# Lightning attention and a low-rank mixer: v's loads on another queue, V's second copy by DMA, some work on other engines and in other steps

## The chip, the cores and the metric

One core of a Trainium2 chip runs the whole kernel. The core has a matmul engine (PE; its weight loads are listed as PEld), a vector engine (DVE, VectorE), a scalar engine (ACT, ScalarE), GpSimd (POOL), and SyncE (SP), which only issues DMAs here. ScalarE can issue DMAs too; each of the two has a queue of its own to the same 16 DMA engines. Times are device microseconds of an execution; lower is better.

## The reference

Inputs: q, k and v of shape (4, 8, 768, 64) in float32, a decay `lam` for each of 8 heads, and U (768 x 32), V (32 x 768), w1 (512 x 2048), w2 (2048 x 512) in float64.

```python
# attention, blocks of 64 positions, per batch and head
intra = ((qb @ kb.T) * Dmask) @ vb          # Dmask[i, j] = lam ** (i - j), i >= j
inter = (qb * lam_pow) @ kv_state
out[block] = intra + inter
kv_state = lam ** 64 * kv_state + (kb * rev_pow).T @ vb
# x: (4, 768, 512), the heads side by side
h = x.transpose(0, 2, 1) @ U @ V            # mixes positions
u = x + h.transpose(0, 2, 1)
result = u + maximum(u @ w1, 0) @ w2
```

## The kernel before, in words

The attention stage runs in 24 steps, one for 128 positions of one batch: step s has batch b = s // 6 and place c = s % 6 in it. The list `pieces` gives the order of the work of all steps, and `run` says what each name does. Every engine takes its instructions in the order in which this list emits them, so the list is the schedule. Steps overlap: step s also turns q and k of step s + 1 (`prep`, L371), computes its scores (`scores`, L403) and masks them on VectorE (`masked`, L413), and finishes step s - 7 (`done`): `mix` (L556) multiplies it with V, `mixed` (L573) adds x, `turn` (L593) transposes the result for the next stage and `store` (L590) writes it to DRAM.

The middle of a step is `intra` (px, L459), `state` (pkv, L431) and `inter` (L470), after which ScalarE copies the result out of PSUM (x_nat, L476). In steps up to 6 `state` comes before `intra`. PSUM has one px tile in this stage, so the next `intra` follows this copy.

Loads run ahead of their use: `prep(s)` ends with the request for the next q, `next_v(s)` (L447), between `state` and `inter`, with the next v, and the end of each step with the next k. There are three buffers each for q and v and four for k, so a load asked for in a step is read about three steps later. q and k are asked for by SyncE, v by ScalarE (the first two by SyncE). The request waits on its engine until the buffer that it fills has been read; what is queued behind it on that engine waits too.

At the end of each batch, `low` (L481) forms U-transposed x as a 128 x 128 tile with four groups g of 32 rows, `low_rows` (L497) then splits it into a high and a low part that lie in the tile vp (as `p_hl`). Its work for the first three batches is in two pieces that `next_of_low` takes up in the first step of the following batch (steps 6, 12 and 18): `own` casts each group on ScalarE (L529) and subtracts on POOL (L530), `other` has SyncE copy each group's rows to its neighbour by four DMAs (L540). `mix` needs both, for the first time in the step after (7, 13 and 19; there it comes after `inter`).

V itself is prepared once, in steps 0 to 5 (`v_steps`, L699): it is fetched as 64-bit words and turned into float32, `five` cuts the low bits off on VectorE (L716), `high` writes this to groups 0 and 2 of `v_hl` with four ScalarE copies (L723), and `low` writes the differences to groups 1 and 3, two subtractions on VectorE and two on POOL (L727). Groups 2 and 3 (rows 64 to 127) hold the same as groups 0 and 1.

Between these, `aside(s)` emits side work listed in `side`: fetches of w1's words (L146, four pieces of 128 KB for each of the first two blocks) and the steps that turn 64-bit words into float32 parts (`one`, L166, and two activations, L173 and L174; `mantissa`, L155; `two`, L184, and so on). The numbers in the list `at` say in which step. What a side step has for ScalarE is kept by `on_scalar` and emitted later, at `late` (in the next step for most; in steps 5 and 6 right after `inter` and `other`).

After the attention stage come the first product (u with w1, L837 and L848) and the second (L969, L971, L973), which run until the end.

Of the kernel before, what the change touches and what calls it, by code (L numbers as in the profile page):

```python
# [8 lines left out]
FP32 = mybir.dt.float32  # L9
# [3 lines left out]
ALU = mybir.AluOpType  # L13
# [5 lines left out]
def kernel(  # L19
# [28 lines left out]
    nc = tc.nc  # L48
# [8 lines left out]
    R = moe_U.shape[1]  # L57
    G = P // R
    SH = S // 2
    NS = B * NT  # L60
# [43 lines left out]
    def tmp(name):  # L104
        return wconv.tile([P, C], FP32, tag="tmp", bufs=2, name=name)
# [149 lines left out]
    def two_banks(name, tag):  # L255
        return psf.tile([P, 2, N], FP32, tag=tag, name=name)
# [7 lines left out]
    def bank(shape, name, tag):  # L264
        return psa[0].tile(shape, FP32, tag=tag, bufs=2, name=name)
# [5 lines left out]
    def parts(s):  # L271
        return 2 if s == 0 else 1
# [20 lines left out]
    v_hl, p_hl = vp[:, 0:S], vp[:, S : S + C]  # L293
# [46 lines left out]
    half = [slice(0, D), slice(D, P)]  # L340
# [105 lines left out]

    def next_v(s):  # L447
        del raw[s, "v"]
        load_next("v", nc.scalar)

    def intra(s):

# [26 lines left out]
    pps = {}  # L479

    def low(b):  # L481

        pp = two_banks("pp", "px")[:, 0, 0:P] if b < B - 1 else bank([P, P], "pp", "b2")
        for c in range(NT):
            for g in range(G):
                nc.tensor.matmul(  # L486
                    out=pp[g * R : (g + 1) * R, :], lhsT=u_w[:, c, :],
                    rhs=xs[b * NT + c][:, g * P : (g + 1) * P],
                    start=(c == 0), stop=(c == NT - 1),
                )  # L490
        if b == B - 1:
            pps[b] = pp
            return
        pps[b] = tmp("p_f")[:, 0:P]
        nc.scalar.copy(pps[b], pp)

    def low_rows(b):  # L497

        pp = pps.pop(b)
        own = [(slice(g * R, (g + 1) * R), slice(g * P, (g + 1) * P)) for g in range(G)]  # L500
        if b == B - 1:
            h, h2, l, l2 = (p_hl[g * R : (g + 1) * R] for g in range(G))
# [12 lines left out]

            def spread_low():
                nc.scalar.copy(l2, l.bitcast(FP32))

            pps[b] = [low_part, spread, spread_low]
            return  # L520


        def place(g, of, low):
            return p_hl[g * R : (g + 1) * R, low * 2 * P + (of % 2) * P :][:, 0:P]

        def own():
            for g in range(G):
                rows, at = pp[g * R : (g + 1) * R], place(g, g, 0)
                nc.scalar.copy(at, rows)  # L529
                nc.gpsimd.tensor_tensor(  # L530
                    out=place(g, g, 1), in0=rows, in1=at.bitcast(FP32), op=ALU.subtract
                )

        def other():
            for g in range(G):
                at, of = (
                    p_hl[x * R : (x + 1) * R].rearrange("r (l h c) -> r l h c", l=2, h=2)
                    for x in (g ^ 1, g)
                )
                nc.sync.dma_start(  # L540
                    out=at[:, :, g % 2].bitcast(FP32), in_=of[:, :, g % 2].bitcast(FP32)
                )

        pps[b] = [own, other]

    def next_of_low(b):
        pps[b].pop(0)()
# [102 lines left out]
    for s in range(NS):  # L650
        b, c = divmod(s, NT)
        done = s - NT - 1
        more = s + 1 < NS
        turns = done > 0 and (done - 1) // TG < FG
        mixes = 0 <= done < NS - NT - 1
        rows = c == 0 and b > 0
        step = [("fade", s)] * (c > 0)
        step += [("mix", done)] * (mixes and c != 1) + [("turn", done - 1)] * turns
        step += [("split", done - 1)] * turns
        step += [("next_of_low", b - 1)] * (s == NT)  # L660
        step += [("prep", s + 1)] * more
        step += [("mix", done + 1)] * (not more)
        step += [("next_of_low", b - 1)] * (rows and s > NT)
        step += [("scale", s + 1)] * more
        step += [("mixed", done)] * (mixes and c != 1)
        step += [("late", s - 1)] * (1 < s < NT - 1 or s > NT)
        step += [("turned", done - 2)] * (done > 1 and c == 1)
        step += [("mixed", done + 1)] * (not more)
        both = [("intra", s), ("state", s)]
        step += (both if s > NT else both[::-1]) + [("next_v", s), ("inter", s)]  # L670
        step += [("next_of_low", b - 1)] * rows
        step += [("late", s)] * (s < 2 or s in (NT - 1, NT))
        step += [("turned", done - 1)] * (done > 0 and c > 0)
# [25 lines left out]
    def v_steps():  # L699

        st = {}

        def dst():
            if "v" not in st:
                st["v"] = wconv.tile([P, C], FP32, tag="wf", name="vf")[0 : 2 * R, 0:SH]
            return st["v"]

        def parts(gs):
            for half in range(2):
                rows, cols = slice(half * R, (half + 1) * R), slice(half * SH, (half + 1) * SH)  # L710
                for g in gs:
                    yield v_hl[g * R : (g + 1) * R, cols], rows

        def five():
            st["t"] = t = wconv.tile([P, C], FP32, tag="wt", name="vt")[0 : 2 * R, 0:SH]
            nc.vector.tensor_scalar(  # L716
                t.bitcast(U32), st["v"].bitcast(U32), HI, None, ALU.bitwise_and
            )
            on_scalar(high)

        def high():
            for out, rows in parts((0, 2)):
                nc.scalar.copy(out, st["t"][rows])  # L723

        def low(g, engine):
            for out, rows in parts((g,)):
                engine.tensor_tensor(  # L727
                    out=out, in0=st["v"][rows], in1=st["t"][rows], op=ALU.subtract
                )

        halves = [moe_V[:, half * SH : (half + 1) * SH] for half in range(2)]
        return weight_steps(dst, halves, SH, 2 * R, in_parts=True) + [
            five, lambda: low(1, nc.vector), lambda: low(3, nc.gpsimd),
        ]


# [3 lines left out]
    side = {}  # L740
    for steps, at in (
        (u_side, (-1, 1, 1, 2, 2)),
        (v_steps(), (0, 0, 3, 3, 4, 4, 4, 5, 5)),
        (w1_steps(0, True, True), (8, 9, 10, 11, 12, 14, 15, 16, 17, 17, 20, 21)),
        (w1_steps(1, True, True), (14, 15, 16, 17, 18, 22, 23, NS, NS, NS, NS, NS)),
    ):
        assert len(steps) == len(at)
        for step, n in zip(steps, at):
            side.setdefault(n, []).append(step)
# [142 lines left out]
    c0, b = NS - NT, B - 1  # L892
# [7 lines left out]
    at = [(1, 5), (1, 17), (2, 4), (2, 17), (3, 3), (3, 10)]  # L900
# [121 lines left out]
    for i in range(len(steps) - STAG):  # L1022
        g, ft = steps[i]
# [49 lines left out]
```

## Time and profile before

| what | value |
|---|---|
| median of 3 runs | 649.1 us (649.07 to 650.27) |
| the profiled execution | 649.85 us, of which span 648.1 us, granted clock 1.000 |
| attention stage | from 0 to about 114.5 us |
| idle PE before 115 us / between 115 and 400 / after 400 us | 4.9 / 0.0 / 3.8 us |
| a steady step (say 74.51 to 78.83, between two runs of L408) | 4.3 us |
| busy ACT / DVE / POOL, whole span | 268.8 / 434.7 / 116.3 us |
| v loads by ScalarE / by SyncE | 22 / 2, 256 KB each, 4.7 us to landing |
| `other` copies (vp<-vp) | 12, 32 KB each, 2.7 us to landing |

The steps' scores (L408) begin as follows: scores(5) at 28.4 us, (6) at 32.2, (7) at 37.5, (8) at 42.0, (12) at 59.4, (13) at 65.2, (14) at 70.1, (18) at 86.9, (19) at 92.8, (20) at 97.5, (23) at 110.6. scores(s) is emitted in step s - 1.

In a row of the timeline the columns are start, duration, engine, line, operation, output<-inputs, shapes and count; brackets hold the engine's idle time before the row and what ended it. An engine with a q (SPq, ACTq) is its sequencer, which issues DMAs; the duration of an issue includes its waiting. In a row of waits the columns are total us, times and the longest.

### The profile page before, as it was taken

The numbers are of one execution on the slowest core, as the hardware profiler recorded it, in microseconds if no ns is written. First come the engines' busy times: TensorE is split into PE (matmuls) and PEld (weight loads), VectorE is DVE, ScalarE is ACT, GpSimd is POOL, SyncE is SP. The second block draws the span as 40 slices with busy tenths as digits, with TensorE's granted clock in tenths as the row PEclk, the third lists the DMA queues.
The fourth block names the chain that finished last, engine by engine and source line by source line (L and its number), as shares of the span: only waits on it lengthen the run. The fifth ranks groups of instructions, "written<-read, shape, count | busy, mean of one in ns | idle before, by whom it ended". The sixth has DMA issues, their size and how long they took to land.

```text
span 648.1 us, 13405 instructions
## 1 busy us (share of the span) xinstructions
PE 639.3 (99%) x5242; PEld 539.3 (83%) x5242; DVE 434.7 (67%) x709; ACT 268.8 (41%) x500; POOL 116.3 (18%) x104
## 2 busy tenths in 40 slices
PE   9899999999999999999999999999999999999997
PEld 8888989788888888888888888888888888888886
DVE  6656878668997777777796244685575665755854
ACT  3675766435755444444454222332322322322320
POOL 4475968330000000000000000030030300300300
PEclk9999999999999999999999999999999999999999
DMA  9979996354876555655587899864363363543521
GB/s 232 241 182 272 231 242 163 119 191 176 287 258 219 209 207 209 207 209 211 211 292 276 320 332 392 287 220 138 96 227 98 123 204 97 172 152 99 179 82 65
DMA packets 132737, 131.69 MB, mean 203 GB/s; under 512 B 81538, under 2 KB 90754, under 8 KB 132674
## 3 DMA queue, kind: packets, MB, share of 16 engines
q1 hardware_dynamic: 107552, 124.41, 59.1%
q10 hardware_dynamic: 25122, 6.42, 4.4%
q8 instruction: 41, 0.67, 0.4%
q14 instruction: 22, 0.18, 0.1%
HBM read 80.09 MB, written 50.33 MB: 201 GB/s over the span
## 4 chain that ended last, share of the span: by engine, by line
PE 97%; ACT 1%; issue 1%; DMA 1%; DVE 0%; ACTq 0%; DVEq 0%
PE pz L837 27%; PE pd L848 13%; PE pz L971 13%; PE pz L969 13%; PE pd L973 13%; PE px L459 4%; PE pss L408 4%; PE px L470 2%; PE pqk L361 2%; PE pkv L431 1%; PE pm L563 1%; PE pp L486 1%; PE pm L626 1%; DMA kraw<-in_k_dram 1%; PE put L604 1%
## 5 line engine op out<-in xcount | busy, mean ns | idle before, releaser
L837 PE MATMUL pz<-u_hl,w 128*128 128x512 f32 x768 | 185.0, 391 | 0.0
L837 PEld LDWEIGHTS pz<-u_hl,w 128*128 128x128 f32 x768 | 143.7, 188 | 30.2 <-ACT r L844 0.6
L971 PE MATMUL pz<-w_hl,m 128*128 128x512 f32 x384 | 148.7, 389 | 0.0
L969 PE MATMUL pz<-w_hl,m 128*128 128x512 f32 x384 | 148.3, 389 | 0.0
L973 PE MATMUL pd<-w_d,m 128*128 128x512 f32 x384 | 147.4, 389 | 0.0
L952 ACT ACTIVATE m<-rm 128x512 fp32r<-128x512 f32 x96 | 60.6, 632 | 182.3 <-PE pd L973 125.5
L953 DVE SCALAR_TENSOR_TENSOR m<-rm,m 128x512 fp32r<-128x512 f32 x96 | 71.6, 748 | 95.7 <-ACT m L952 95.7
L998 POOL TENSOR_TENSOR o<-o,u 128x512 f32<-128x512 f32 x20 | 29.8, 1523 | 433.1 <-DVE o L994 433.1
L853 DVE SCALAR_TENSOR_TENSOR r<-pd,r 128x512 f32<-128x512 f32 x96 | 61.7, 685 | 60.4 <-ACT r L844 48.2
L848 PE MATMUL pd<-u_d,w 128*128 128x512 f32 x384 | 95.7, 390 | 0.0
L971 PEld LDWEIGHTS pz<-w_hl,m 128*128 128x128 f32 x384 | 72.1, 188 | 15.0
L969 PEld LDWEIGHTS pz<-w_hl,m 128*128 128x128 f32 x384 | 72.1, 188 | 15.0
L973 PEld LDWEIGHTS pd<-w_d,m 128*128 128x128 f32 x384 | 72.1, 188 | 14.7
L848 PEld LDWEIGHTS pd<-u_d,w 128*128 128x128 f32 x384 | 72.0, 188 | 14.9
L844 ACT ACTIVATE r<-pz 128x512 f32<-128x512 f32 x96 | 51.7, 591 | 66.9 <-PE pz L837 66.9
L954 DVE SCALAR_TENSOR_TENSOR m<-m 128x512 fp32r<-128x512 f32 x96 | 74.7, 779 | 3.0
L417 DVE TENSOR_TENSOR sm<-pss,mask 128x512 f32<-128x512 f32 x48 | 30.9, 686 | 18.0 <-PE pss L408 17.8
L215 ACT ACTIVATE w<-wf 128x512 fp32r<-128x512 f32 x32 | 20.3, 633 | 36.5 <-DVE wf L197 28.7
L173 ACT ACTIVATE sc<-sc,ends 128x512 f32<-128x512 uint32 x30 | 21.6, 721 | 22.8 <-DVE sc L166 22.8
L459 PE MATMUL px<-vraw,sm 128*64 128x64 f32 x768 | 29.0, 228 | 1.6 <-issue 1.4
L408 PE MATMUL pss<-qt,kt 64*128 64x128 f32 x384 | 29.0, 290 | 0.6 <-issue 0.5
L459 PEld LDWEIGHTS px<-vraw,sm 128*64 128x64 f32 x768 | 25.9, 140 | 3.4 <-issue 2.5
(91 smaller groups left out, 606.6 us busy)
## 6 DMA issues: line engine op xcount, KB each, us to landing
r_d<-r SPq DMA_DIRECT2D x96, 256.0 KB, 2.5
rm<-r_d SPq DMA_DIRECT2D x96, 256.0 KB, 2.7
words<-in_moe_w_ch_dram SPq DMA_DIRECT2D x30, 512.0 KB, 4.2
w_d<-w SPq DMA_DIRECT2D x16, 768.0 KB, 3.4
w_hl<-w_d SPq DMA_DIRECT2D x16, 512.0 KB, 6.2
u_d<-x_nat SPq DMA_DIRECT2D x24, 256.0 KB, 4.4
u<-u_d SPq DMA_DIRECT2D x24, 256.0 KB, 4.5
qraw<-in_q_dram SPq DMA_DIRECT2D x23, 256.0 KB, 4.8
```

The lines of the kernel that those rows point to most:

```text
L408: nc.tensor.matmul(out=pss[:, x, a, :], lhsT=kt[half[x], a, :], rhs=qt[half[x], a, :], start=True, stop=True,)
L459: nc.tensor.matmul(out=px[half[t], x, a, :], lhsT=sm[:, x, a, half[t]], rhs=vr[:, 2 * a + x, :], start=(a == 0), stop=(alone and a == HP - 1),
L837: nc.tensor.matmul(out=like(acc[g][0], g), lhsT=w[:, n, ct, :], rhs=columns(uhl[g][:, n], g, ct), start=(ct == 0 and n == 0), stop=(ct == ...
L844: nc.scalar.mul(rs[g], acc[g][0], 4096.0 + 1.0)
L848: nc.tensor.matmul(out=like(acc[g][1], g), lhsT=w[:, 2, ct, :], rhs=columns(ud[g], g, ct), start=(ct == 0), stop=(ct == CT - 1),)
L853: nc.vector.scalar_tensor_tensor(rs[g], acc[g][1], 4096.0, rs[g], ALU.mult, ALU.add)
L952: nc.scalar.activation(out=m[:, 0], in_=r, func=AF.Relu, scale=NEAR)
L953: nc.vector.scalar_tensor_tensor(m[:, 1], r, 0.0, hi, ALU.max, ALU.subtract)
L954: nc.vector.scalar_tensor_tensor(m[:, 2], hi, E, low, ALU.mult, ALU.subtract)
L969: nc.tensor.matmul(out=pz, lhsT=m[:, 0, cols], rhs=hl[:, 0], start=first, stop=False)
L971: nc.tensor.matmul(out=pz, lhsT=m[:, 1, cols], rhs=hl[:, 1], start=False, stop=end)
L973: nc.tensor.matmul(out=pd, lhsT=m[:, 2, cols], rhs=dd, start=first, stop=end)
```

## The change

- `next_v` asks SyncE, not ScalarE, for v. The request stands at the same place in the list. (The third load of v, before step 0, stays with ScalarE.)
- `own` for the first batch is as before. For the second and third batch POOL subtracts groups 0 and 1 alone, and a new piece, `own_rest`, subtracts groups 2 and 3 on VectorE. It has a place of its own in steps 6, 12 and 18, after `mixed`, and does nothing in step 6.
- V: `high` makes two copies and not four, `low` two subtractions on VectorE and none on POOL. A new piece, `again`, has SyncE copy rows 0 to 63 of `v_hl` (192 KB) to rows 64 to 127. It is kept for `late` by `aside(5)`, so it is emitted in step 6 after `next_v` and `other`.
- w1's first block is fetched in steps 6, 7, 9 and 11 and not 8 to 11; the second in 18 to 21 and not 14 to 17, and its `one` is in step 22 and not 18.

```diff
     def next_v(s):
         del raw[s, "v"]
-        load_next("v", nc.scalar)
+        load_next("v")
...
+        def low(engine, gs):
+            for g in gs:
+                engine.tensor_tensor(
+                    out=place(g, g, 1), in0=pp[g * R : (g + 1) * R],
+                    in1=place(g, g, 0).bitcast(FP32), op=ALU.subtract,
+                )
+
         def own():
             for g in range(G):
-                rows, at = pp[g * R : (g + 1) * R], place(g, g, 0)
-                nc.scalar.copy(at, rows)
-                nc.gpsimd.tensor_tensor(
-                    out=place(g, g, 1), in0=rows, in1=at.bitcast(FP32), op=ALU.subtract
-                )
+                nc.scalar.copy(place(g, g, 0), pp[g * R : (g + 1) * R])
+                if g < 2:
+                    low(nc.gpsimd, [g])
+            if b == 0:
+                low(nc.gpsimd, [2, 3])
+
+        def own_rest():
+            if b > 0:
+                low(nc.vector, [2, 3])
...
-        pps[b] = [own, other]
+        pps[b] = [own, own_rest, other]
...
         step += [("mixed", done)] * (mixes and c != 1)
+        step += [("next_of_low", b - 1)] * rows
         step += [("late", s - 1)] * (1 < s < NT - 1 or s > NT)
...
         def high():
-            for out, rows in parts((0, 2)):
+            for out, rows in parts(0):
                 nc.scalar.copy(out, st["t"][rows])
 
-        def low(g, engine):
-            for out, rows in parts((g,)):
-                engine.tensor_tensor(
+        def low():
+            for out, rows in parts(1):
+                nc.vector.tensor_tensor(
                     out=out, in0=st["v"][rows], in1=st["t"][rows], op=ALU.subtract
                 )
+            on_scalar(again)
+
+        def again():
+            nc.sync.dma_start(out=v_hl[half[1]].bitcast(FP32), in_=v_hl[half[0]].bitcast(FP32))
...
-        (v_steps(), (0, 0, 3, 3, 4, 4, 4, 5, 5)),
-        (w1_steps(0, True, True), (8, 9, 10, 11, 12, 14, 15, 16, 17, 17, 20, 21)),
-        (w1_steps(1, True, True), (14, 15, 16, 17, 18, 22, 23, NS, NS, NS, NS, NS)),
+        (v_steps(), (0, 0, 3, 3, 4, 4, 4, 5)),
+        (w1_steps(0, True, True), (6, 7, 9, 11, 12, 14, 15, 16, 17, 17, 20, 21)),
+        (w1_steps(1, True, True), (18, 19, 20, 21, 22, 22, 23, NS, NS, NS, NS, NS)),
```

More of the change, by code (lines that the diff above doesn't have):

```diff
@@ L706, in dst, with parts @@
             return st["v"]
[L708 to L712, printed above, removed]
+        def parts(g):
+            for i in range(2):
+                rows, cols = slice(i * R, (i + 1) * R), slice(i * SH, (i + 1) * SH)
+                yield v_hl[g * R : (g + 1) * R, cols], rows
         def five():
@@ L721, in high @@
         def high():
-            for out, rows in parts((0, 2)):
+            for out, rows in parts(0):
                 nc.scalar.copy(out, st["t"][rows])
-        def low(g, engine):
-            for out, rows in parts((g,)):
-                engine.tensor_tensor(
+        def low():
+            for out, rows in parts(1):
+                nc.vector.tensor_tensor(
                     out=out, in0=st["v"][rows], in1=st["t"][rows], op=ALU.subtract
                 )
-        halves = [moe_V[:, half * SH : (half + 1) * SH] for half in range(2)]
+            on_scalar(again)
+        def again():
+            nc.sync.dma_start(out=v_hl[half[1]].bitcast(FP32), in_=v_hl[half[0]].bitcast(FP32))
+        halves = [moe_V[:, i * SH : (i + 1) * SH] for i in range(2)]
         return weight_steps(dst, halves, SH, 2 * R, in_parts=True) + [
-            five, lambda: low(1, nc.vector), lambda: low(3, nc.gpsimd),
+            five, low,
         ]
```

## The prediction

> **What bounds the kernel now.** I read the page's busy table first, then the waits of the matmul engine, then the timeline around each wait, then the DMA queues in the stretches before the waits.
>
> ```profile
> span 648.1 us, 13405 instructions
> PE 639.3 (99%) x5242; PEld 539.3 (83%) x5242; DVE 434.7 (67%) x709; ACT 268.8 (41%) x500; POOL 116.3 (18%) x104
> q1 hardware_dynamic: 107552, 124.41, 59.1%
> q10 hardware_dynamic: 25122, 6.42, 4.4%
> q8 instruction: 41, 0.67, 0.4%
> ```
>
> PE is busy for 639.3 of 648.1 us, so 8.8 us is all that any change off PE can win. The table by windows puts 4.9 us of idle PE before 115 us (the attention stage, the only one that the diff touches) and 3.8 us after 400 us, which the diff cannot reach. q10 is ScalarE's DMA queue, almost all of it v's loads; q1 is SyncE's; q8 brings PE's instructions in blocks of 16 KB.
>
> ```profile
> PE px L459 <- issue: 1.4, 4, 0.4
> PE pqk L361 <- issue: 1.2, 2, 0.9
> PE pss L408 <- issue: 0.5, 1, 0.5
> PE pqk L361 <- DMA kraw<-in_k_dram: 0.2, 1, 0.2
> PE pkv L431 <- issue: 0.2, 1, 0.2
> ```
>
> No row says that PE waits for ScalarE's DMA issues, for POOL or for v. "issue" means that the profile shows no wait. Six of these gaps lie inside a run of equal matmuls, for example:
>
> ```profile
> 20.30 0.49 PE L408 MATMUL pss<-qt,kt 64*128 64x128 f32 x4 [0.49 <-issue]
> 25.78 0.40 PE L361 MATMUL pqk<-ident,kraw 64*128 64x64 f32 x7 [0.90 <-issue]
> 92.10 0.34 PE L459 MATMUL px<-vraw,sm 128*64 128x64 f32 x4 [0.43 <-issue]
> ```
>
> The six end at 20.30, 25.78, 35.30, 54.44, 63.99 and 92.10 us and hold 2.49 us (0.49, 0.90, 0.26, 0.18, 0.23, 0.43). Before each, a q8 block ends (18.82, 24.30, 33.87, 53.06, 62.53, 90.70), always 1.38 to 1.48 us earlier, and the instruction counts at which they happen differ by multiples of about 256. So PE ran out of instructions. Counting the trace's PE records in blocks of 256, a block starts to move 1.0 to 3.05 us after PE enters the one before it, and PE stalls where that exceeds about 2.2 to 2.6 us. The two longest delays (20.3 to 23.35 and 86.7 to 89.74) have much v traffic in them, the two shortest (64.1 to 65.26 and 92.2 to 93.22) none. The rows are the DMA queues in the two long stretches and in the first short one; the last column is the share of 16 DMA engines:
>
> ```profile
> q1 hardware_dynamic: 2227, 0.56, 82.9%
> q10 hardware_dynamic: 755, 0.19, 28.1%
> ...
> q1 hardware_dynamic: 2080, 0.60, 85.6%
> q10 hardware_dynamic: 748, 0.19, 28.7%
> ...
> q1 hardware_dynamic: 1049, 0.27, 102.1%
> ```
>
> Against it: 30.6 to 32.97 us took 2.4 us with q10 at only 5.4%, and 49.7 to 52.1 us took 2.4 us with about 9%.
>
> The last thing to see is what the first mix waits for (step 7):
>
> ```profile
> 35.61 0.37 SPq L282 DMA_DIRECT2D qraw<-in_q_dram  x1
> 36.08 3.28 SPq L540 DMA_DIRECT2D vp<-vp  x4
> 37.42 0.38 ACTq L282 DMA_DIRECT2D vraw<-in_v_dram  x1
> 37.52 0.97 PEld L408 LDWEIGHTS pss<-qt,kt 64*128 64x128 f32 x16 [0.28 <-ACT kt L367]
> 41.78 0.50 PE L563 MATMUL pm<-vp 64*128 64x256 f32 x4
> ```
>
> The four small copies of `other` leave from 36.08 us and land at 39.85, 40.03, 40.96 and 41.14; mix(0) starts at 41.78. It has 0.64 us to spare.
>
> **The change part by part.**
>
> *v's loads on SyncE.* 22 issues of 0.38 us (8.4 us) leave ScalarE's queue. There they lie between pkv's end and the end of inter, where ScalarE waits for PE anyway (0.4 to 1.1 us idle before x_nat): worth 0. On SP each step has five issues instead of four, some 0.4 to 0.6 us each of a 4.3 us step. The v issue waits for px and pkv of its step, and behind it now stand, in order, `other` (steps 6, 12, 18), the words, `store` and k. `store` waits for mixed() until about that time anyway. k leaves up to 2.6 us later in steps 1 to 6 (25.43 becomes about 28.2), but is read three steps later against 4.7 us to land; v3 moves from 11.26 to about 14.1, lands near 19 and is read at 21.28. Without that slack each late load would cost its lateness; I take 0, bounds 0 to +0.5.
>
> *V's second half by a DMA.* ScalarE loses 2 copies of 0.51 us at L723, POOL loses 2 of 1.00 us at L727. The ScalarE copies end at 34.79, but p_f behind them reads pp, which PE ends at 34.71, so kt and pss(7) come only 0.06 us earlier: -0.05, bounds -0.15 (the whole PE gap there) to 0. The price is the new copy, `again`. It is queued by aside(5), but sent with late(6), behind v9 and all of `other`. In SP's order: v9 when px(6) ends, 37.42; then four issues at the spacing of 0.65 that the rows of `other` show: 37.85, 38.5, 39.15, 39.8; then `again` at 40.5. For its time to land the rows give 1.84 (the last `other` at 95.33) as the low end, 2.04 (a store of 256 KB in a quiet stretch, 114.32) as the nearest in size, 2.7 (median of `other`), and 4.9 (V's words in full traffic) as the high end. I take 2.1, plus 0.2 as a share of a block of q8 in its way (one of 16 engines was late by 0.5 to 1.3 us in all four `other` copies behind the q8 block at 37.22): it lands at 42.8, mix(0) wants it at 41.75, so PE stalls about 0.95. Bounds +0.6 (landing at 42.35) to +3.6 (45.4). I call it +0.9. The `other` copies themselves now leave about as late as 39.8 and land near 41.7: no further cost, as `again` lands after them.
>
> *Low parts of turns 1 and 2 on VectorE.* POOL loses 4 of 12 subtractions of 0.45 to 0.69 us. VectorE gains 4; the nearest row is L508, 32x128, 0.29 us. Step 12: ScalarE's casts of g2 and g3 end at 65.2 and 65.5, so VectorE ends at 65.87 instead of being free; then kv 0.42, L166 0.42, and masked(13) starts at 66.72 instead of 66.40, px(13) 0.3 later. But mix(6) waited there: its four matmuls take 0.70 us (69.61) against 0.40 usually, because the last `other` lands at 69.71. `other` still ends its issues at about 67.5, now because v15 stands ahead rather than POOL. So 0.3 is lost and 0.3 not waited for: 0, bounds -0.2 to +0.3. Step 18: L166 leaves this step, masked(19) is not delayed (93.78 against pss's end at 93.99): +0.05, bounds 0 to +0.3.
>
> *Words in other steps.* w1(0)'s first two pieces go to steps 6 and 7 (behind `again`), w1(1)'s four to 18 to 21, `one` of w1(1) from 18 to 22. L166 there is 0.43 us and VectorE is idle for 1.01 us before masked(23): 0; without that gap it would cost 0.43. The two exponent activations (0.72 each) move to step 23, between 112.9 and x_nat at 114.53: they fit in 1.64 us of idle ScalarE: 0, bounds 0 to +0.2.
>
> *PE's instructions.* With v on q1, a q8 block competes with one data queue and not two. If the delay then never exceeds the 2.43 that the stretches with little v show, the stalls at 20.30 and 92.10 go (0.49 and about 0.3 of 0.43, the rest being eaten by masked(19)), the one at 25.78 shrinks by 0.7, the one at 54.44 stays, and those at 35.30 and 63.99 are worth nothing, since PE would then wait for kt (37.48) and sm(13) instead. That is -1.5. If the queue is not the cause, 0; and worse is possible, as k and words bunch up behind v, +0.3. The correlation has two clear rows for and two against, so I take half: -0.75, bounds -1.9 (all but the two covered) to +0.3. [...]
>
> Sum: 0 - 0.05 + 0.9 + 0.05 + 0 - 0.75 = +0.15. The profiled execution took 649.85 us (span 648.1 and 1.75 around it), 0.75 over the median of 649.1. It becomes 650.0; as a median, 649.25, so 649.3.
>
> **The rivals.**
>
> *B: v's queue makes no difference to the instruction blocks.* For: 2.4 us of delay with 5.4% of q10. Against: 3.05 and 3.02 only with 28%. The sum is +0.9: 650.0.
>
> *C, slower: `again` comes late and the stalls stay.* Place: mix(0) in step 7, PE's order being fixed. If a q8 block or k10 and the words hold one DMA engine as they did `other` (0.5 to 1.3 us), it lands at 43.4 to 44: a stall of 1.7 to 2.2. It decides from a landing at about 43.2. For: the block at 41.78 takes 1.69 us, just then. Against: the DMA share is only 0.56 in the window 35 to 40 us. About +1.8: 650.9.
>
> *D, faster: the stalls go and `again` lands at 42.2.* -1.9 and +0.45: 647.6. For: two of the stalls sit where v's traffic is densest. Against: 54.44.
>
> **How the numbers follow.** The forecast A (both terms about as sized) 0.42, B 0.23, C 0.20, D 0.15. A measurement of this kernel tells 0.2%, 1.3 us, from no change. D is faster, with 0.02 of A: 0.17. C is slower, with 0.08 of B (a somewhat later `again`) and 0.02 of A: 0.30. The rest, 0.53, lies within. A's own range is 648.4 to 650.4. For 8 in 10 the range reaches to the middle of D and past that of C: 647.6 to 651.2.
>
> **What would show it.** Right: a gap of about 0.9 us before the first L563 in step 7, released by a DMA of vp; no "issue" gap at about 20 and 92, a smaller one near 25; px(13) some 0.3 later after sm(13) and no long mix(6); no PE wait for vraw or kraw. Wrong: mix(0) starting without a wait (`again` left or landed sooner), the six gaps unchanged or moved to other counts, or a PE wait for a load behind v in SP's queue.

## The result, and the profile after

The change makes the kernel slower: 660.1 us (median of 4 runs, 658.3 to 662.0) against 649.7 us (649.1 to 650.6), a ratio of 1.0162 with a 95% interval of 1.0132 to 1.0192. The prediction said 649.3 us, in 647.6 to 651.2.

The page of the profiled execution after (661.41 us): the span, the busy row of the engines, the granted clock in 40 slices of 16.5 us, and three DMA queues.

```profile
span 659.6 us, 13401 instructions
PE 643.6 (98%) x5242; PEld 543.0 (82%) x5242; DVE 437.5 (66%) x713; ACT 268.0 (41%) x498; POOL 113.0 (17%) x98
PEclk9989898999999999999999999999999999999999
q1 hardware_dynamic: 129472, 130.12, 61.5%
q10 hardware_dynamic: 3282, 0.92, 0.6%
q8 instruction: 41, 0.67, 0.4%
```

The span is 11.5 us longer. PE is idle for 12.13 us before 130 us, where it was 4.86; that is 7.3. The other 4.3 us are in PE's busy time (643.6 against 639.3) with the same 5242 matmuls: three 8s in the clock row, where before had none in this stage. In three stretches, from 44.0 us for 6.8 us, from 74.7 for 3.4 and from 105.4 for 3.4, the granted clock is 0.5. This is one execution; the mean granted clocks of the four are 0.989, 0.994, 0.988 and 0.997, so this part differs between them. v's traffic has gone from q10 to q1 as asked.

The waits of PE over the span (total us, times, the longest):

```profile
PE pm L574 <- DMA vp<-vp: 4.5, 2, 3.6
PE px L459 <- ACT u_hl L651: 2.8, 2, 2.4
PE px L459 <- ACT x_nat L476: 1.8, 1, 1.8
```

There are three places: the first mix (step 7), px of step 13, px of step 19. In step 7 the timeline shows SyncE's issues and the mix's matmuls:

```profile
32.24 2.16 SPq L282 DMA_DIRECT2D qraw<-in_q_dram  x1
...
36.32 2.25 SPq L282 DMA_DIRECT2D qraw<-in_q_dram  x1
38.66 0.87 SPq L282 DMA_DIRECT2D vraw<-in_v_dram  x1
39.63 3.29 SPq L551 DMA_DIRECT2D vp<-vp  x4
43.00 0.55 SPq L744 DMA_DIRECT2D vp<-vp  x1
...
44.47 0.55 PE L574 MATMUL pm<-vp 64*128 64x256 f32 x1 [3.57 <-DMA vp<-vp]
...
45.99 0.76 PE L574 MATMUL pm<-vp 64*128 64x256 f32 x3 [0.98 <-DMA vp<-vp]
```

`other` (L551) leaves at 39.63 and not at 36.08, though POOL has its low parts ready at 36.73. Its first copy lands at 44.16, 0.17 us after the v load that SyncE issued just ahead of it (43.99); `again` (L744) leaves at 43.00 and lands at 45.91. PE waits 3.57 us for the one and then 0.98 for the other.

Steps 13 and 19 wait for something else. Step 12 in the kernel before, on POOL, VectorE and PE (the last row is px of step 13):

```profile
64.63 2.27 POOL L530 TENSOR_TENSOR vp<-p_f,vp 32x128 fp32r<-32x128 f32 x4 [4.64 <-ACT vp L529]
65.64 0.42 DVE L166 TENSOR_SCALAR sc<-words 128x512 uint32<-128x512 uint32 x1
66.40 1.29 DVE L417 TENSOR_TENSOR sm<-pss,mask 128x512 f32<-128x512 f32 x2 [0.34 <-PE pss L408]
66.98 1.28 POOL L392 TENSOR_TENSOR qs<-qt,powq 128x512 f32<-128x512 f32 x1
67.19 1.24 PE L459 MATMUL px<-vraw,sm 128*64 128x64 f32 x32
```

The same step after:

```profile
70.28 0.96 POOL L528 TENSOR_TENSOR vp<-p_f,vp 32x128 fp32r<-32x128 f32 x2 [4.57 <-ACT vp L535]
70.93 1.81 DVE L528 TENSOR_TENSOR vp<-p_f,vp 32x128 fp32r<-32x128 f32 x2 [0.62 <-POOL vp L528]
71.32 1.27 POOL L392 TENSOR_TENSOR qs<-qt,powq 128x512 f32<-128x512 f32 x1
72.55 1.10 POOL L381 TENSOR_TENSOR ks<-kraw,small 128x512 f32<-128x512 f32 x1
72.77 0.42 DVE L437 COPY kv<-px 128x256 f32<-128x256 f32 x1
73.22 0.71 DVE L166 TENSOR_SCALAR sc<-words 128x512 uint32<-128x512 uint32 x1
73.86 1.27 DVE L417 TENSOR_TENSOR sm<-pss,mask 128x512 f32<-128x512 f32 x2
```

VectorE's two subtractions take 1.81 us together: 0.46 for the first and 1.32 for the second, which ends 0.15 us after POOL's multiplication qs does. L166 takes 0.71 and not 0.42, and ends 0.28 us after POOL's next one, ks. kv and the x_nat copy behind it, L166 and `masked` all come later by that, and PE waits 2.40 us (to 74.64) before px(13). POOL, which has two subtractions fewer, starts qs 1.04 us after its first subtraction begins, where it was 2.35.

### The profile page after: what moved, and what is told of

Its sections match the earlier page's. It is cut to its first block, busy times and chain, and to the rows that moved or that the text cites. A ratio compares the mean times of both kernels' runs of the same rounds, so it can differ in the third digit from the quotient of the medians.

```text
span 659.6 us, 13401 instructions
## 1 busy us (share of the span) xinstructions
PE 643.6 (98%) x5242; PEld 543.0 (82%) x5242; DVE 437.5 (66%) x713; ACT 268.0 (41%) x498; POOL 113.0 (17%) x98
## 4 chain that ended last, share of the span: by engine, by line
PE 91%; DMA 4%; DVE 1%; SPq 1%; POOL 1%; issue 1%; ACT 1%; DVEq 0%; POOLq 0%; ACTq 0%
PE pz L852 27%; PE pd L863 13%; PE pz L986 13%; PE pz L984 13%; PE pd L988 13%; PE px L459 3%; PE pss L408 2%; DMA kraw<-in_k_dram 2%; PE px L470 2%; PE pqk L361 1%; SPq L282 1%; PE pkv L431 1%; PE pm L574 1%; DMA qraw<-in_q_dram 1%; PE put L615 1%
## 5 line engine op out<-in xcount | busy, mean ns | idle before, releaser
L969 DVE SCALAR_TENSOR_TENSOR m<-m 128x512 fp32r<-128x512 f32 x96 | 74.7, 779 | 3.0
L392 POOL TENSOR_TENSOR qs<-qt,powq 128x512 f32<-128x512 f32 x20 | 25.5, 1275 | 27.7 <-ACT qt L367 27.5
```

The lines of the kernel that those rows point to most:

```text
L969: nc.vector.scalar_tensor_tensor(m[:, 2], hi, E, low, ALU.mult, ALU.subtract)
```

## The experiments

Each ratio is to the kernel before, run beside it on the same chip. "Gap" is the idle time of PE ahead of an instruction in the profiled execution.

### One part undone

**v back on ScalarE** (the rest of the change kept):

```diff
-        load_next("v")
+        load_next("v", nc.scalar)
```

> The changed kernel with v asked for by ScalarE again, all else as changed. Theory Q (SyncE's queue is backed up by v's loads, so the four copies of `other` leave at 39.6 us and land at 44.2 to 44.5): `other` leaves at about 36 to 39 us, the stall of 3.57 us before the first mix goes, about 0.9 us for `again` stays, and the half clock after it (44.0 to 50.8 us) goes. The stalls of 2.40 and 1.79 us in steps 13 and 19 stay, and PE's code stalls (2.5 us in the kernel before, 0.4 in the changed one) come back: about 655 us. Rival C (`again` alone makes the first mix wait): the stall in step 7 stays above 3 us and the time stays within 1 us of 660.

654.5 us, ratio 1.0064 (1.0043 to 1.0084). `other` leaves at 35.67, `again` at 39.08 and lands at 42.10, and the mix's gap is 0.48 us. The gaps of 2.40 and 1.78 in steps 13 and 19 stay. So v's queue is the cause in step 7, and about 1.0% of the 1.6%.

**All subtractions back on POOL:**

```diff
-                if g < 2:
-                    low(nc.gpsimd, [g])
-            if b == 0:
-                low(nc.gpsimd, [2, 3])
+                low(nc.gpsimd, [g])
         def own_rest():
-            if b > 0:
-                low(nc.vector, [2, 3])
+            pass
```

> The changed kernel with all four low parts subtracted by GpSimd again. Theory P (VectorE's subtraction, with both inputs in SBUF, is held up by GpSimd's qs multiplication): the stalls of 2.40 and 1.79 us in steps 13 and 19 and the half clock after each (3.4 us long, some 1.5 us lost each) go, under 0.5 us stays: about 653 us; step 7 is as in the changed kernel. Rival Q2 (those stalls too come from `other` behind v on SyncE): both stay, about 660 us.

657.4 us, 1.0109 (1.0072 to 1.0146): a smaller gain than expected. The gap of step 19 is gone (0.11), that of step 13 is not (2.38). It has a second cause there, which stood behind the first: L166, ahead of `masked` on VectorE, waits 1.83 us for words.

```profile
68.28 1.26 POOL L392 TENSOR_TENSOR qs<-qt,powq 128x512 f32<-128x512 f32 x1
68.60 1.22 DVE L166 TENSOR_SCALAR sc<-words 128x512 uint32<-128x512 uint32 x1 [1.83 <-DMA words<-in_moe_w_ch_dram]
```

The words left at 64.38, behind a v load whose issue took 2.35 us. Coming late, L166 also meets qs, takes 1.22 us and ends 0.28 us after it. The mix's gap in step 7, which this edit doesn't touch, is 2.01 us here; among the kernels with v on SyncE it differs a good deal.

**V's second half by engines again** (the old `high`, `low` and step list; no `again`):

```diff
-        (v_steps(), (0, 0, 3, 3, 4, 4, 4, 5)),
+        (v_steps(), (0, 0, 3, 3, 4, 4, 4, 5, 5)),
```

> The changed kernel with V's four ScalarE copies and two GpSimd subtractions again, no `again`. Theory Q: the first mix still waits some 3.5 us for `other`, the second wait of 0.98 us goes: 658 to 659.5 us. Rival C: the stall in step 7 goes down to under 1 us and the clock stays full there: 653 us.

658.9 us, 1.0129 (1.0090 to 1.0169). The mix's gap falls from 3.57 + 0.98 to 2.51 + 0.11: `again` adds to the wait but doesn't make it.

**Words in their old steps:**

```diff
-        (w1_steps(0, True, True), (6, 7, 9, 11, 12, 14, 15, 16, 17, 17, 20, 21)),
-        (w1_steps(1, True, True), (18, 19, 20, 21, 22, 22, 23, NS, NS, NS, NS, NS)),
+        (w1_steps(0, True, True), (8, 9, 10, 11, 12, 14, 15, 16, 17, 17, 20, 21)),
+        (w1_steps(1, True, True), (14, 15, 16, 17, 18, 22, 23, NS, NS, NS, NS, NS)),
```

> The changed kernel with w1's words fetched in their old steps. Theory: the words hardly matter, all three stalls stay: 659 to 661 us. Rival: the words in steps 6 and 7, or 18 to 21, are what delays `other` and the loads: a stall in step 7 shorter by over 1 us, 657 us or less.

665.0 us, 1.0225 (1.0190 to 1.0259): a miss. With v on SyncE the old words steps are worse by 0.6% (the two intervals just meet); px of step 19 waits 3.20 us. The move of the words seems to be worth something, but only in the state that v's move creates.

### One part alone on the kernel before

**v on SyncE alone:** the diff of the first experiment, the other way round, on the kernel before.

> The kernel before with v asked for by SyncE, nothing else. Theory Q: SyncE's queue backs up (issues of 1.3 to 2.3 us with no semaphore left to wait for), `other` of step 6 leaves near 39 to 40 us, the first mix waits 2 to 3.5 us; the words of step 11 land too late for `one` in step 12 and px(13) waits up to 2.4 us, as in the run with GpSimd's subtractions put back; PE's code stalls fall from 2.5 to under 1 us: 653 to 656 us. Rival (only together with `again` and the words is the queue full): no stall over 1 us, and with the code stalls gone 647.5 to 649.5 us.

658.1 us, 1.0110 (1.0054 to 1.0166): the direction as expected, the size larger. SyncE and the mix in step 7:

```profile
36.88 2.04 SPq L282 DMA_DIRECT2D vraw<-in_v_dram  x1
39.02 2.92 SPq L540 DMA_DIRECT2D vp<-vp  x4
...
42.22 0.35 PE L563 MATMUL pm<-vp 64*128 64x256 f32 x1 [0.42 <-DMA vp<-vp]
...
44.52 0.50 PE L563 MATMUL pm<-vp 64*128 64x256 f32 x3 [1.95 <-DMA vp<-vp]
```

The v issue takes 2.04 us, `other` leaves 2.9 us later than before, and its copies land at 41.91, 42.08, 44.30 and 44.48. The 2.2 us between the second and the third are not v's, which landed at 41.74: of the 256 packets of the four copies 248 have ended by 42.90, and the last eight follow one another from 43.20 to 43.67, at the end of a q8 block that moves from 42.28 to 43.21. Whether the block held them up is not shown: the trace doesn't number the engines, and no run here moves the block. The longer wait, 1.95 us, ends at 44.52 with the fourth copy, the shorter, 0.42, at 42.22 after the second. Steps 13 and 19 have gaps of 2.39 (late words) and 2.48.

**VectorE's subtractions alone:**

```diff
-        pps[b] = [own, other]
+        pps[b] = [own, own_rest, other]
...
+        step += [("next_of_low", b - 1)] * rows
```

with `low`, `own` and `own_rest` of the change.

> The kernel before with the low parts of groups 2 and 3 of the second and third batch on VectorE, nothing else. Theory P: each second subtraction takes about 1.3 us instead of 0.3, behind GpSimd's qs; px(13) and px(19) wait 2.4 and 1.8 us, and most executions lose a stretch of half clock on top: 653 to 656 us. Rival (the stalls there need v on SyncE): no wait over 0.5 us, 649 to 650.5 us.

654.5 us, 1.0068 (1.0045 to 1.0090), as expected. Gaps of 1.62 (step 13) and 2.41 (step 19).

**`again` alone**, the V part of the change:

```diff
-        (v_steps(), (0, 0, 3, 3, 4, 4, 4, 5, 5)),
+        (v_steps(), (0, 0, 3, 3, 4, 4, 4, 5)),
```

> The kernel before with V's second half copied by a DMA, nothing else. With v on ScalarE the copy leaves at about 39.1 us and lands at 42.1, as in the run with v put back: the first mix waits about 0.5 us, no half clock: 649.5 to 651 us. Rival: it is what breaks step 7, over 2 us there: 652 us or more.

651.3 us, 1.0021 (0.9998 to 1.0043). `again` leaves at 38.88, lands at 41.57 and costs a gap of 0.29.

**Words alone**, the two lists of w1:

```diff
-        (w1_steps(0, True, True), (8, 9, 10, 11, 12, 14, 15, 16, 17, 17, 20, 21)),
-        (w1_steps(1, True, True), (14, 15, 16, 17, 18, 22, 23, NS, NS, NS, NS, NS)),
+        (w1_steps(0, True, True), (6, 7, 9, 11, 12, 14, 15, 16, 17, 17, 20, 21)),
+        (w1_steps(1, True, True), (18, 19, 20, 21, 22, 22, 23, NS, NS, NS, NS, NS)),
```

> The kernel before with w1's words in the new steps, nothing else. Theory: fetches of 128 KB in other steps of a queue with room change nothing but which code block PE waits for: within 1.3 us of the kernel before. Rival: with v on ScalarE they already make `other` or a load late, a wait over 1 us in steps 7, 13 or 19.

650.3 us, 0.9998 (0.9975 to 1.0020): nothing.

**`again` and the words together**, without v's move and VectorE's subtractions (the first two experiments' edits in one):

```diff
-        load_next("v")
+        load_next("v", nc.scalar)
...
-            if b > 0:
-                low(nc.vector, [2, 3])
+            pass
```

> The changed kernel with v on ScalarE and all subtractions on GpSimd: `again` and the words alone. Theory (v's queue and VectorE's subtractions are all of the loss): no wait over 0.6 us, no half clock, 649 to 651.5 us, a ratio of 0.999 to 1.003. Rival (the parts need each other): over 652 us.

651.3 us, 1.0010 (0.9994 to 1.0026). So v's move and the subtractions are the whole loss. Alone they cost 1.10% and 0.68%, 1.78% in sum; the change as a whole lost 1.62%. In step 13 both delay the same px, which fits, but the intervals are too wide to show the difference.

### Inside v's move: a held queue, or a place behind v

The trace lets one count, at each issue of SyncE, how many packets of q1 issued before it are not yet finished. In the kernel before, q1 is nearly empty between 29.7 and 43 us (0 to 1,084 packets when an issue of a load begins) and these load issues take 0.37 to 0.58 us. After, from 24 to 39 us, 8 issues of 11 begin with 1,900 to 2,213, about two loads of 1,024 packets; those take 0.77 to 2.25 us each. The three longest (2.24, 2.16, 2.25) end when 214, 124 and 271 are left. Their buffers were free: the q load at 36.32, say, needs PE's reading of q7, which ended at 34.68. The kernel before has the same: the words at 44.68 take 1.87 us, with 2,087 unfinished.

That gives two theories: the hold of SyncE's issues itself (Q), and the place of the small copies behind v's 1,024 packets in one queue (F).

**v on SyncE and k on ScalarE**, so that SyncE's queue has as many loads as before:

```diff
-        "next_k": lambda s: load_next("k"),
+        "next_k": lambda s: load_next("k", nc.scalar),
```

> v asked for by SyncE as in the run of that part alone, and in exchange k asked for by ScalarE: each queue has as many loads as before. Theory Q (SyncE's queue cannot hold three loads a step, so its issues are held up): `other` of step 6 leaves within 1.5 us of the end of GpSimd's subtractions, no wait over 1 us before the first mix, none over 1 us for late words in step 13: 649 to 652 us. Rival W (it is v's wait for PE, standing in SyncE's order ahead of `other` and the words, that makes them late): the stalls stay as with v alone (1.95, 2.39, 2.48 us), 656 to 658 us.

655.8 us, 1.0066 (1.0044 to 1.0088): neither theory alone. Step 7:

```profile
39.99 0.37 SPq L282 DMA_DIRECT2D vraw<-in_v_dram  x1
...
40.45 3.00 SPq L540 DMA_DIRECT2D vp<-vp  x4
...
45.29 0.80 PE L563 MATMUL pm<-vp 64*128 64x256 f32 x4 [0.26 <-DMA vp<-vp]
```

v's issue here is back to 0.37 us, the mix's gap is 0.26, and no words come late. But the mixes of steps 13 and 19 now wait 1.33 and 1.44 us for `other`. In the first of them `other` left at 69.25 and landed at 73.97, 0.17 us after the v load that was issued at 68.78. This execution, the slowest of its seven, also has a stall of 1.92 us at 22.92, 1.44 us after a q8 block, with 3.4 us of half clock behind it, so not all of the 0.66% need be F.

**v on SyncE, `other` ahead of v:**

```diff
-        step += (both if s > NT else both[::-1]) + [("next_v", s), ("inter", s)]
-        step += [("next_of_low", b - 1)] * rows
+        step += both if s > NT else both[::-1]
+        step += [("next_of_low", b - 1)] * rows + [("next_v", s), ("inter", s)]
```

> The kernel before with v's loads asked for by SyncE (b1, 1.0110), and in steps 6, 12 and 18 the four copies of `other` asked for ahead of the step's v load and not behind it. Theory F (the copies wait in the queue behind v's 1,024 packets): the first copy no longer lands with v, the waits of the mix steps (b1: 0.42 and 1.95 us at step 7) fall under 0.4 us, while the waits in steps 13 and 19 (2.39 and 2.48 us, late words and kt) stay: about 655 us, 1.008. Theory Q (SyncE's issues are held while some 2,000 packets are unfinished, wherever `other` stands): the loads queued ahead of `other` hold it as they held v, the mix still waits over 1 us: 657 to 658 us, as b1.

660.1 us, 1.0131 (1.0084 to 1.0177). No mix waits any more, as F said (the first copy leaves at 34.82 and lands at 39.52, 0.16 us after the q load that is ahead of it now), but the time doesn't fall. Steps 13 and 19 now have gaps of 4.62 and 3.39 us. Step 12:

```profile
67.47 1.28 DVE L166 TENSOR_SCALAR sc<-words 128x512 uint32<-128x512 uint32 x1 [4.01 <-DMA words<-in_moe_w_ch_dram]
68.67 1.27 DVE L417 TENSOR_TENSOR sm<-pss,mask 128x512 f32<-128x512 f32 x2
...
69.44 0.80 PE L459 MATMUL px<-vraw,sm 128*64 128x64 f32 x10 [4.62 <-issue]
```

The words left at 63.20, behind a v load that left at 61.73 and landed at 67.00, and landed at 67.34. L166 waits for them, and `masked` stands behind L166. The queue takes from the next thing in it what the copies no longer pay.

**Both: k on ScalarE and `other` ahead of v** (the last two diffs in one).

> The kernel of d1 (v on SyncE, `other` ahead of v) with k asked for by ScalarE too, so that SyncE's queue has as many loads as before. If the hold of SyncE's issues and the place behind v are together the whole price of v's move, no wait over 0.6 us is left in the mix steps or in steps 13 and 19, and the time is that of before: 649 to 651 us, where c1 (k alone) gave 655.8 and b1 658.1. If a third cause is there, 653 to 656 us.

653.6 us where before was 651.5, 1.0033 (1.0002 to 1.0063): two thirds of v's 1.10% are back. The largest gap for a late copy is 0.17 us, and no words are late. What is left in the profiled execution are stalls of 2.19 us (22.97) and 1.93 (78.78), each ending 1.3 to 1.5 us after a block of q8 has come in. Stalls of that kind come and go in kernels with v on either queue: one of 2.28 us stands at 27.60 in the kernel with only `again` and the words. So Q and F together are most of the price of v's move; whether the last 0.3% belongs to it, these runs leave open.

### Inside VectorE's subtractions

**One input from PSUM** (the subtraction's kind and place in VectorE's order as in the kernel with the subtractions alone, its data not; as it no longer reads the cast, it doesn't wait for ScalarE either):

```diff
-                low(nc.vector, [2, 3])
+                for g in (2, 3):
+                    nc.vector.tensor_tensor(
+                        out=place(g, g, 1), in0=last_pt[0][g * R : (g + 1) * R, 0, 0:P],
+                        in1=pp[g * R : (g + 1) * R], op=ALU.subtract,
+                    )
```

> The kernel before with the two low parts of the second and third batch on VectorE, but with one input of each read from PSUM (old scores' input, so that these low parts are not the right numbers; the work and its place are the same). Theory P: with one SBUF input VectorE is not held up by GpSimd, each takes about 0.3 to 0.45 us, px(13) and px(19) wait under 0.6 us, no half clock: 649.5 to 651.5 us. Rival (they are long because they wait for ScalarE's casts and stand in front of masked): the second still lasts 1.3 us, waits of 1.6 to 2.4 us, 654 us.

651.7 us, 1.0021 (1.0002 to 1.0039). Step 12:

```profile
62.88 0.62 DVE L546 TENSOR_TENSOR vp<-pqk,p_f 32x128 fp32r<-32x128 f32 x2
63.86 1.28 POOL L394 TENSOR_TENSOR qs<-qt,powq 128x512 f32<-128x512 f32 x1
63.98 1.44 DVE L166 TENSOR_SCALAR sc<-words 128x512 uint32<-128x512 uint32 x1
66.12 1.06 PE L461 MATMUL px<-vraw,sm 128*64 128x64 f32 x26 [1.35 <-ACT kt L369]
```

The subtractions fall to 0.31 us each. But without the wait for the casts they are over (63.50) before qs begins (63.86): they ran beside POOL's own subtractions, and the run does not show that PSUM would have freed them beside qs. A gap of 1.35 stays: now qs meets L166, which takes 1.44 us and not 0.42, and again ends (65.42) a little after qs (65.14).

**qs behind `masked`:** the subtractions alone, and in steps 12 and 18 POOL copies one column of the masked scores before it begins qs.

```diff
+    def scale_after(s):
+        seen = att.tile([P, 1], FP32, tag="seen", bufs=1, name="seen")
+        nc.gpsimd.tensor_copy(out=seen, in_=st[s]["sm"][:, 0, 0, 0:1])
+        scale(s)
...
-        step += [("scale", s + 1)] * more
+        step += [("scale", s + 1)] * (more and not (rows and s > NT))
...
-        step += [("masked", s + 1)] * more
+        step += [("masked", s + 1)] * more + [("scale_after", s + 1)] * (rows and s > NT)
```

> The kernel before with VectorE's subtractions (b2, 1.0068, waits of 1.62 and 2.41 us before px of steps 13 and 19), and in steps 12 and 18 GpSimd's qs is held until VectorE has masked the first half of the scores (a copy of one column on GpSimd makes it wait), so that GpSimd has no instruction beside VectorE's subtractions, kv and L166. Theory L (GpSimd's qs locks VectorE out): the second subtraction falls from 1.32 to 0.3 to 0.5 us, L166 stays at 0.42, each wait falls under 0.6 us: 650 to 651 us, within 0.3% of before. Theory S (the subtractions take that long on VectorE by themselves, or their place ahead of kv is the cost): waits stay over 1.3 us, 653 to 655 us. If qs now comes too late, a wait of inter (L470) for qs appears instead, and its size tells.

1.0009 (0.9982 to 1.0035): the loss is gone. Step 12:

```profile
64.45 0.78 DVE L533 TENSOR_TENSOR vp<-p_f,vp 32x128 fp32r<-32x128 f32 x2 [0.61 <-POOL vp L533]
65.74 0.43 DVE L166 TENSOR_SCALAR sc<-words 128x512 uint32<-128x512 uint32 x1
67.18 1.00 PE L464 MATMUL px<-vraw,sm 128*64 128x64 f32 x24
67.22 0.18 POOL L398 COPY seen<-sm 128x1 f32<-128x1 f32 x1 [2.46 <-DVE sm L422]
67.36 1.28 POOL L392 TENSOR_TENSOR qs<-qt,powq 128x512 f32<-128x512 f32 x1
```

The same two subtractions, with both inputs in SBUF, take 0.78 us, L166 0.43, and px(13) has only 0.09 us of gap; step 19 keeps 0.87. The subtractions themselves were never dear. Dear was that POOL, relieved of two of them, began qs some 1.3 us earlier in the step, beside the part of VectorE's work that `masked` stands behind.

### The half clock

**The change with 16 idle matmuls ahead of the first mix's own:**

```diff
+            for i in range(16 if s == 0 else 0):
+                nc.tensor.matmul(out=pm[:, 0, 0:P], lhsT=ident, rhs=ident, start=True, stop=True)
```

> The changed kernel with 16 matmuls of no use (128x128x128 on the identity, into columns that mix(0) overwrites) ahead of the first mix, where PE waits 3.57 us. Theory H (PE's clock is halved because PE idled): the wait before the first mix falls to under 1 us, the half clock from 44.0 to 50.8 us goes, those in steps 13 and 19 may stay; 2 to 3 us less than the changed kernel: 657 to 658.5 us. Rival (half clock has another cause, or the useless matmuls cost as much): the half clock stays, or the time is 660 us or more.

659.9 us, 1.0150 (1.0126 to 1.0174), not to be told from the change itself. Two stretches of the kernel after (busy PE, PEld, DVE, ACT, POOL; then granted clock, DMA share, GB/s), and the same two with the idle matmuls:

```profile
42.00:47.00 5.00, 1.55 (x10) 1.32 (x12) 0.20 (x1) 0.65 (x3) 0.00 (x0) 0.70 0.61 138
47.00:52.00 5.00, 5.00 (x94) 4.82 (x91) 3.06 (x5) 1.67 (x3) 1.07 (x1) 0.62 1.07 274
```

```profile
42.00:47.00 5.00, 4.39 (x47) 4.10 (x46) 0.51 (x1) 1.03 (x4) 0.00 (x0) 1.00 0.59 134
47.00:52.00 5.00, 5.00 (x140) 4.68 (x138) 3.32 (x7) 2.90 (x8) 2.76 (x3) 1.00 0.99 252
```

With PE kept at work the clock stays at 1.00, and 138 weight loads fit where 91 did. So the slow stretch after step 7 follows PE's idling. This execution has no half clock in steps 13 and 19 either, though its waits there are 2.42 and 1.79 us.

The trace of the kernel after shows how much PE idled ahead of each stretch. The granted clock changes there at 44.00, 50.83, 74.72, 78.14, 105.44 and 108.86 us, and these times lie 2, 7, 1, 8 and 1 times 3.413 us apart. In pieces of that length, counted from them, three at full clock before 130 us hold 3.10, 2.40 and 1.79 us of idle PE (the ends of matmuls are modelled), and half clock follows each of the three; the others at full clock hold 0.50 or less, in the kernel before 0.90 or less, and half clock follows none. At half clock 1.44 us (step 7, 44.00 to 47.41) was followed by 3.4 us more of it. The length of the wait alone does not settle it: the waits of 2.40 and 1.79 us in steps 13 and 19 of the kernel after were each followed by 3.4 us at half clock, those of 2.42 and 1.79 with the idle matmuls by none. What tells them apart is not shown.

In time it is worth little more than the idle matmuls cost: the profiled span is 657.7 against 659.6 us.

### All of it mended

**The whole change, with k on ScalarE, `other` ahead of v, and qs behind `masked`** (the three diffs above in one).

> The whole change with three things mended: k asked for by ScalarE, `other` ahead of v, GpSimd's qs after masked in steps 12 and 18. If these are all that made the change slower, 649.5 to 652 us (what c4 gave, 651.3, with the two parts undone), and no wait over 1 us before 130 us except `again` before mix(0). If the parts have a further price together, 654 us or more.

659.0 us where before was 651.5, 1.0100 (1.0065 to 1.0134): the second of the expected outcomes. Steps 13 and 19 wait 1.09 and 0.78 us, but `again` now comes very late:

```profile
37.95 3.56 SPq L556 DMA_DIRECT2D vp<-vp  x4
41.60 0.54 SPq L282 DMA_DIRECT2D vraw<-in_v_dram  x1
42.23 0.54 SPq L749 DMA_DIRECT2D vp<-vp  x1
...
47.21 0.50 PE L579 MATMUL pm<-vp 64*128 64x256 f32 x3 [3.06 <-DMA vp<-vp]
```

`other` ahead of v puts v's issue at 41.60, since it waits for POOL's subtractions, and `again` behind that. It takes 4.93 us to land (47.16), where it took 3.02 with v on ScalarE, and a half-clock stretch of 3.4 us follows from 48.8. v itself landed at 44.65, so its place behind v is not the whole of it. Of the 64 packets of `again` 60 have ended by 45.33, and the last four follow one another from 45.43 to 46.36; a q8 block moves from 44.18 to 45.44. As in the kernel with v alone on SyncE, the last packets end after such a block, and whether it held them up is not shown. The times spread more (652.5 to 661.5) than those of the change.

No version here beats the kernel before; those not to be told from it are the words alone, `again` alone or with the words, and the subtractions with qs moved.

## Why the prediction was wrong

**v's loads on SyncE, taken as 0 with bounds 0 to +0.5: this step failed.** Alone it cost 1.10% (0.54 to 1.66), some 7 us. ScalarE's side held. On SyncE's side the sum priced every issue at 0.4 to 0.6 us, from rows with an almost empty queue, and so had `other` leave from 37.85 and v9 as v9 leaves from ScalarE. In fact v9 left at 38.66, held up by issues of up to 2.25 us ahead of it, and `other` at 39.63. The rows to see it were in the trace of before: the words at 44.68 take 1.87 us, with 2,087 packets unfinished. The question to ask was not how long an issue takes but how full the queue is when a third load per step joins it.

**"No further cost, as `again` lands after them" failed as well.** It followed from the departure of 37.85. The first copy of `other` landed at 44.16 and cost 3.57 us before `again` came into it. It was not priced that the copies would land behind v, although only v's queue changed; the traces show them 0.17 us behind v, in the change and in the run with k on ScalarE.

**`again`, +0.9 with bounds +0.6 to +3.6: about right as a mechanism.** Alone it costs a gap of 0.29, with v on ScalarE 0.48 in the rest of the change, and 0.98 in the change itself. That this last one is so near the 0.95 of the working is luck: `again` left at 43.00 and not at 40.5. It landed in 2.7 to 3.0 us where 2.3 was taken, in the middle of the bounds. Rival C named the right place, mix(0), and the right sign, but with `again` as its cause and 1.8 us as its price. The condition that it named, a q8 block that holds one DMA engine, is not shown: with v alone on SyncE (43.20 to 43.67, packets of `other`) and with all mended (45.43 to 46.36) the last packets end after such a block, and no run moves the block.

**Low parts on VectorE, 0 and +0.05 with bounds to +0.3: this step failed.** Alone they cost 0.68%. The 0.29 us came from L508, whose input pp is in PSUM; here both inputs, p_f and vp, are in SBUF. Without POOL beside it the subtraction does take about 0.3 to 0.46 us, as the run with qs moved shows, so the size of the work was right. What was missed is that POOL's freed time brings qs forward against VectorE, and that VectorE's instruction beside qs then ends only after it (0.15 us in the kernel after). Two kinds of instruction took longer beside qs: the subtraction 1.32 us against 0.3 to 0.46, and L166 1.44 against 0.42. `masked`, with one input in PSUM, took its usual 1.29 us beside it (the kernel before). The prediction took the subtraction's time from a row and did not ask what POOL would do meanwhile.

**Words, 0: right** alone (0.9998). With v on SyncE they were worth 0.6% the good way, which no step had.

**PE's instructions, -0.75: not borne out.** The stalls at q8's blocks before 130 us did fall in the profiled execution, from 2.49 to 0.41 us. But they vary as much with v on either queue: with v on ScalarE from next to nothing (the words alone) to 4.1 us (the subtractions with qs moved: 0.42, 0.26, 1.06, 1.58 and 0.73), with v on SyncE from 0.4 to 4.5 (k on ScalarE and `other` ahead of v: 2.19, 1.93 and 0.36). v's queue is not shown to matter. The correlation was read from a handful of stretches of a single execution. What the choice of queue did cost lies elsewhere: 22 loads moved from ScalarE's queue to SyncE's cost 1.10% alone, where issues on SyncE took up to 2.73 us and the copies of `other` left 2.9 us later than before.

**The sum** was +0.15 us and came out at +10.4. Of the 11.5 us in the span, 4.3 are slower matmuls, a term that the sum did not have at all. An estimate from these rows: 4.3 us over 13.65 us at half clock is some 1.1 for 3.4 us, so the wait of 2.40 us in step 13 cost about 3.5 with the stretch behind it.

**The forecast's signs of error** were of use. "`again` late" showed at the named place; "px(13) some 0.3 later" showed as 2.4, which pointed at the second cause at once.

## What to carry to other kernels

Price a DMA moved to another engine by how many packets its new queue already has unfinished when it is issued, and by what small, urgent copies then stand behind it; here the 0.4 to 0.6 us of an issue into an almost empty queue said nothing of the 0.77 to 2.25 us with 1,900 packets or more. When work is taken off GpSimd, ask what it will start sooner, and what VectorE does in that stretch: here a subtraction with two inputs in SBUF took 1.32 us beside qs and not 0.3 to 0.46, a pass from SBUF to SBUF 1.44 and not 0.42, so look at the inputs, and at what runs beside, before taking a duration from a row. And undo the parts one by one: here two parts cost 1.1% and 0.7%, one stood behind the other in one step, and a third looked useless until they were there.

## What the hardware showed unexpectedly

- In the stretches counted, SyncE's issue of a load takes 0.37 to 0.58 us while its queue has under 1,100 packets unfinished (the kernel before, 29.7 to 43 us), 0.71 to 0.87 at 1,135 to 1,249, and 0.77 to 2.25 from 1,900 on (the kernel after, 24 to 39 us); the three longest of these end with 124 to 271 left, and with v alone on SyncE one takes 2.73 us. The count does not fix the time: in the kernel after one takes 0.61 us with 2,091 unfinished (45.63) and one 0.39 with 1,898 (60.70).
- VectorE beside GpSimd's qs: a subtraction of 32 x 128 took 1.32 us and not 0.3 to 0.46, and a one-input pass over 128 x 512 took 1.44 and not 0.42, each ending 0.15 to 0.3 us after GpSimd's qs (the subtraction in the kernel after, the pass in the run with an input from PSUM). The masking pass, with one input in PSUM, ran beside qs in its usual 1.29.
- In the kernel after, half clock came in stretches of 6.83, 3.41 and 3.41 us, each behind a piece of 3.41 us with 3.10, 2.40 and 1.79 us of idle PE; behind pieces with 0.90 us or less, here and in the kernel before, came none up to 130 us. A wait of 2.40 us in step 13 was followed by 3.4 us at half clock there, and one of 2.42 with the idle matmuls by none.
- Small copies late after a q8 block of 16 KB (PE's instructions): with v alone on SyncE the last eight of `other`'s 256 packets ended 0.8 us after the rest (43.67 against 42.90), the block at 43.21, and PE waited 1.95 us. No run moves the block.
